# Loading the FFN's first weights ahead of the query weights in a one-core decode kernel

## The chip, the cores and the metric

The kernel runs on one core of a Trainium2 chip. The core has five engines, each with its own stream of instructions: TensorE (PE), which multiplies matrices and writes its results to PSUM; VectorE (DVE); ScalarE (ACT); GpSimd (POOL); and SyncE (SP), which here does nothing but issue DMA transfers. The engines wait for each other, and for transfers, through semaphores. Sixteen DMA engines carry data from HBM to the on-chip memory (SBUF). Transfers issued by one engine go through one queue.

The metric is device time in microseconds (us) of one execution; lower is better. The median of 3 runs of the kernel before is 675.64 us (675.47 to 675.78).

## The reference

One decoding step for two sequences: attention over a long cache, beside a small FFN, mixed by a gate. The cut version:

```python
B, D = 2, 448;  H, Sk, Dh = 16, 4096, 256;  F = 1792      # all float32

g = sigmoid((x * gate_w).sum(-1))                          # x: [B, 1, D]
q = (x @ wq) as [B, H, 1, Dh]                              # wq: [D, H*Dh]
p = softmax(q . k_cache * Dh**-0.5)                        # k_cache, v_cache: [B, H, Sk, Dh]
a = (p . v_cache) as [B, 1, H*Dh] @ wo                     # wo: [H*Dh, D]
h = relu(x @ w1 + b1) ** 2                                 # w1: [D, F]
b = h @ w2 + b2                                            # w2: [F, D]
out = g * a + (1 - g) * b                                  # [B, 1, D]
```

The caches are 134 MB each, and every byte of them is used once. wq is 7.3 MB, w1 and w2 3.2 MB each, wo 7.3 MB.

## The kernel before

**Rounds.** The cache is worked through in 16 rounds. A round is one sequence and two heads (`rounds`, `of_round`): its keys are a tile of 128 partitions by 64 KB, its values likewise. Keys go in turn to two buffers, `kp[0]` and `kp[1]`; values go to one buffer, `vp` (the last rounds use `kp` as well).

**One round's work.** The vector engine multiplies the keys with the round's query, which lies copied to all partitions (`times_q`, L439), and sums each row (`row_sums`, L444). Each is done in two halves of 128x8192 elements, so a round has four long vector instructions (`rest`). `maximum` takes the largest score: a vector reduction, two PE matmuls that carry it to all partitions of a head, and a second reduction in `softmax`, after which ACT takes the exponentials into `pw`. `values` (64 matmul instructions) multiplies `pw` with the values. The query tile of a round is made by `make_q`: two PE matmuls pick a row of `qs` and spread it, and ACT copies it out of PSUM to one of three tiles.

**Queue of loads.** All large loads are issued by SP through `load` (L271), in the order in which the program writes them. SP waits before an issue until the place that the transfer overwrites has been read for the last time, and whatever is written behind waits as well. So the keys of round i + 2 wait until the vector engine has ended round i, because they share a buffer, and the values of round i + 1 until PE has ended `values` of round i.

**The start.** wq, w1 and the first values all use `vp`, one after the other. SP's order is: wq (L300), the keys of round 0 (`load_k(0)`, L399), w1 (L424), the keys of round 1 (L433), and then, in the loop of L638, values of round 0, keys of round 2, values of round 1, keys of round 3. Meanwhile ACT issues small loads of x, gate_w, b2 and b1 (L309 to L321) in its own queue, into a corner of `kp[1]`. From x a small PE matmul and four vector instructions make `xT` (L367 to L373), the operand by which `times_x` (L375) multiplies wq or w1. Then PE has three more small matmuls in its order: the gate's (L390), b2's (L392) and b1's (L394); b1's writes the PSUM bank `ph`, which the vector engine reads at L395. After these, PE multiplies with wq (L421, into the bank `po1`), ACT copies the result to `qs` (L422), the first two queries are made (L425, L426), and PE multiplies with w1 (L429, into the bank `ph`); ACT copies that to `shared` (L431). `ffn_turn` (L634) transposes it on PE after the first softmax, and `ffn_square` (L648) adds b1, squares and gates it in the first pass of the loop.

**The order of work on an engine** is the order in which the program writes its operations (`op`). Waits are worked out from the places that each operation reads and writes. PE runs rounds 0 to 11 in hardware loops of four passes (`flow.loop`); the vector engine, ACT and SP have them written out.

**The end.** The last rounds, the projection by wo and the FFN's second layer follow, with w2 loaded last of all.

Of the kernel before, what the change touches and what calls it, by code (L numbers as in the profile page):

```python
# [6 lines left out]
AF = mybir.ActivationFunctionType  # L7
# [3 lines left out]
PE, ACT, DVE, POOL, SP = "PE", "ACT", "DVE", "POOL", "SP"  # L11
# [12 lines left out]
class Flow:  # L24
# [22 lines left out]
    def op(self, eng, fn, r=(), w=(), give=None, take=(), dma=None):  # L47
        proc = dma or eng
        looped = eng == PE and self.body is not None
        o = Op(proc, eng, fn, give, looped)  # L50
        mine = self.ops.setdefault(proc, [])
        mine.append(o)
        o.n = len(mine)
        know = self.know[eng]
        for t in take:
            p = self.tokens[t].pop(0)
            o.takes.append((t, 16 if p.proc not in self.eng else 1))
            self.learn(know, p)
        need = {}
        for writes, regions in ((False, r), (True, w)):  # L60
            for name, lo, hi in map(self.span, regions):
                for p, a, b, wrote in self.seen.setdefault(name, []):
                    if a >= hi or b <= lo or not (wrote or writes):
                        continue
                    if p.proc == proc == PE:
                        continue
                    if know.get(p.proc, 0) < p.n and need.get(p.proc, p).n <= p.n:
                        need[p.proc] = p
        for p in sorted(need.values(), key=lambda p: -p.n):
            if know.get(p.proc, 0) >= p.n:  # L70
                continue
            assert not looped, (eng, p.proc, p.n, r, w)
            while p.give and p.proc in self.eng:
                later = [q for q in self.ops[p.proc][p.n:] if not q.give and q is not o]
                assert later, (eng, p.proc, p.n, r, w)
                p = later[0]
            p.inc = True
            o.waits.append(p)
            self.learn(know, p)
        for writes, regions in ((False, r), (True, w)):  # L80
            for name, lo, hi in map(self.span, regions):
                at = self.seen.setdefault(name, [])
                if writes:
                    at[:] = [x for x in at if not (lo <= x[1] and x[2] <= hi)]
                at.append((o, lo, hi, writes))
        o.know = dict(know)
        if give:
            self.tokens.setdefault(give, []).append(o)
        if looped:
            if self.passes == 1:  # L90
                self.body.append(o)
            else:
                first = self.body[self.at]
                assert first.takes == o.takes and not o.waits, (first.takes, o.takes)
                self.at += 1
        else:
            self.order[eng].append(o)
        return o
# [84 lines left out]
def gated_mix_kernel(nc, x, k_cache, v_cache, wq, wo, w1, b1, w2, b2, gate_w, out):  # L183
    P = 128
    B, H, S, DH = k_cache.shape
    D = x.shape[-1]
    F = w1.shape[1]
    N = H * DH
    XR = 7
# [10 lines left out]
    QB = 512  # L200
    NQ = N // QB
# [11 lines left out]
    scale = DH ** -0.5  # L213

    flow = Flow(nc)
    op = flow.op

    def sb(name, *shape):
        return nc.alloc_sbuf_tensor(name, shape, F32).ap()

    def bank(name):
        return nc.alloc_psum_tensor(name, (P, 512), F32).ap()
# [3 lines left out]
    vp = sb("vp", P, NK * DH)  # L226
# [10 lines left out]
    xT = sb("xT", P, 2, XC, 2, B)  # L237
# [5 lines left out]
    qs = sb("qs", P, QB)  # L243
# [14 lines left out]
    po_t = [bank(f"po{n}") for n in range(2)]  # L258
# [7 lines left out]
    def rows(t):  # L266
        return t.rearrange("p (j d) -> p j d", d=DH)

    def load(eng, sem, dst, src, w, r=(), give=None):
        e = flow.eng[eng]  # L270
        op(eng, lambda: e.dma_start(dst, src), r=r, w=w, dma=sem, give=give)  # L271

    def place(t, lo=0, hi=NK * DH):
        return ("vp" if t is vp else "kp1" if t is kp[1] else "kp0", lo, hi)
# [7 lines left out]
    def of_round(src, i):  # L282
        b, n = rounds[i]
        return src[b, 2 * n:2 * n + 2].rearrange("h (p j) d -> (h p) j d", p=PH)

    def load_k(i, lo=0, hi=NK):
        t = kp[i % 2]
        load(SP, f"k{i % 2}_{lo}", rows(t)[:, lo:hi, :], of_round(k_cache, i)[:, lo:hi, :], [place(t, lo * DH, hi * DH)])
# [7 lines left out]
        return t  # L296

    by7 = "(r k) (s n) -> (r k s) n"
    wq_t = vp[:, :D * N // P]
    load(SP, "wq", wq_t, wq.rearrange(by7, k=XR, s=2).rearrange("(p k) n -> p (k n)", k=XR), [place(vp, 0, D * N // P)])  # L300

    start_at = kp[1][:B, :4 * D + XC * P]

# [19 lines left out]
    v_, s_, t_, g_ = nc.vector, nc.scalar, nc.tensor, nc.gpsimd  # L323
# [36 lines left out]
    def mms(calls):  # L360
        def run():
            for out_, lhsT, rhs, start, stop in calls:
                i = t_.matmul(out_, lhsT, rhs, start=start, stop=stop, skip_group_check=True)  # L363
            return i
        return run

    op(PE, mms([(pxv[:, c, :], xr[:, c].rearrange("b r s -> b (r s)"), ident[:B, :B], True, True) for c in range(XC)]),  # L367
       r=[xr_r, "ident"], w=["sm"])
# [6 lines left out]
    def times_x(out_, t, width, n):  # L375
        calls = []
        for a in range(XR):
            c, half = divmod(a, 2)
            for k in range(n):
                calls.append((out_[32 * k:32 * k + 2 * B, :width], xT[:, half, c].rearrange("p s b -> p (s b)"),  # L380
                              t[:, (a * n + k) * width:(a * n + k + 1) * width], a == 0, a == XR - 1))
        return mms(calls)
# [20 lines left out]
    def col(i):  # L403
        b, n = rounds[i]
        a, k = divmod(n, NQ // 2)
        r = 32 * k + B * a + b
        return ident[:, r:r + 1]

    def make_q(i, token=False):
        c = sel if token else col(i)  # L410
        op(PE, mms([(pq[k * PH:(k + 1) * PH, :DH], c.to_broadcast([P, PH]), qs[:, k * DH:(k + 1) * DH], True, True)
                    for k in range(2)]), r=["qs", "sel" if token else "ident"], w=["pq"], take=["q"] if token else ())
        t = q_t[i % 3]
        q_of[i] = t
        op(ACT, lambda: s_.activation(t, pq[:, :DH], AF.Copy), r=["pq"], w=[f"q{i % 3}"])  # L415
# [2 lines left out]
        c = col(i)  # L418
        op(ACT, lambda: s_.activation(sel, c, AF.Copy), r=["ident"], w=["sel"], give="q")

    op(PE, times_x(po_t[1], wq_t, QB, NQ // 2), r=["xT", place(vp, 0, D * N // P)], w=["po1"])  # L421
    op(ACT, lambda: s_.activation(qs, po_t[1], AF.Copy, scale=scale), r=["po1"], w=["qs"])  # L422
    w1_t = vp[:, :D * F // P]
    load(SP, "w1", w1_t, w1.rearrange(by7, k=XR, s=2).rearrange("(p k) n -> p (k n)", k=XR), [place(vp, 0, D * F // P)])  # L424
    make_q(0)  # L425
    make_q(1)  # L426

    h_sb = shared[:2 * B, :F // 2]
    op(PE, times_x(ph, w1_t, D, FB // 2), r=["xT", place(vp, 0, D * F // P)], w=["ph"])  # L429
    for k in range(FB // 2):  # L430
        op(ACT, lambda k=k: s_.activation(h_sb[:, k * D:(k + 1) * D], ph[32 * k:32 * k + 2 * B, :D], AF.Copy),  # L431
           r=["ph"], w=[("shared", k * D, (k + 1) * D)])
    load_k(1)  # L433

    def times_q(i, half, lo, hi):
# [320 lines left out]
```

## Time and profile before

| what | value |
|---|---|
| median of 3 runs | 675.64 us (675.47 to 675.78) |
| the profiled execution | 675.83 us, of which the span from its first to its last instruction is 674.4 us |
| DMA, share of 16 engines, large loads | 99.3% |
| moved | 289.73 MB, mean 430 GB/s |
| vector engine busy | 571.1 us (85%) |
| PE busy | 254.9 us (38%) |
| ACT busy | 43.5 us (6%) |
| mean granted clock of TensorE | 0.656 |

The profile is one execution. All its times count from the first instruction. A line of its timeline has the start in us, the duration in us, the engine, the line of the kernel, the operation, the tile written and the tiles read, and the number of instructions that were merged; in square brackets stands the engine's idle time just before and what ended it. "SPq" or "ACTq" marks the issue of a transfer; its duration is that of the issuing instruction, not of the transfer. Most PE instructions have the line L363, which is that of a helper: they are told apart by their tiles. w1 and w2 both show as `in_B_w_dram`, b1 and b2 as `in_B_b_dram`. "PEld" is the loading of a matmul's stationary operand. A line of the view by stretches has the stretch, its length, each engine's busy time and number of instructions, then the granted TensorE clock, the mean busy share of the 16 DMA engines, and GB/s.

### The profile page before, as it was taken

What the parts mean: (1) busy time and instruction counts of PE and PEld (TensorE: products, weight loads), DVE (VectorE), ACT (ScalarE), POOL (GpSimd) and SP (SyncE); (2) the same over time, 40 slices, a digit from 0 to 9 for tenths busy, and PEclk for the clock granted to TensorE, in tenths of its full rate; (3) what the DMA queues carried; (4) which work ended last, traced back from release to release, by engine and by line L of the source; (5) the groups of instructions that cost most, each with busy time, mean ns of one, the idle gap of its engine ahead of it and who ended that gap; (6) DMA issues with size and microseconds to landing.
All of it is one profiled execution on the core that took longest, in us unless ns stands there. A gap on an engine that the chain in (4) does not pass through costs nothing.

```text
span 674.4 us, 3918 instructions
## 1 busy us (share of the span) xinstructions
PE 254.9 (38%) x1716; PEld 87.4 (13%) x1716; DVE 571.1 (85%) x147; ACT 43.5 (6%) x145; POOL 0.7 (0%) x6
## 2 busy tenths in 40 slices
PE   2612350512305761140505455050321580421598
PEld 1100210100001510010101311010000140000223
DVE  3069999999999895989979896897979899999930
ACT  0001000010100201010000201000010110000000
POOL 0000000000000000000000000000000000000000
PEclk9957585655758577585856578565575856565789
DMA  9999999999999999999999999999999999999997
GB/s 382 428 439 436 436 435 435 435 435 436 435 435 431 424 436 435 435 435 435 435 435 431 424 436 435 435 431 435 435 435 435 415 445 435 435 436 435 410 438 325
DMA packets 6679, 289.73 MB, mean 430 GB/s; under 512 B 766, under 2 KB 908, under 8 KB 1548
## 3 DMA queue, kind: packets, MB, share of 16 engines
q1 hardware_dynamic: 6616, 289.54, 99.3%
q8 instruction: 9, 0.15, 0.1%
q10 hardware_dynamic: 52, 0.02, 0.0%
q14 instruction: 2, 0.02, 0.0%
HBM read 289.56 MB, written 0.01 MB: 429 GB/s over the span
## 4 chain that ended last, share of the span: by engine, by line
DMA 43%; DVE 26%; PE 3%; SPq 0%; issue 0%; DVEq 0%
DMA kp<-in_A_k_cache_dram 26%; DVE s L444 13%; DVE kp L439 13%; DMA vp<-in_A_v_cache_dram 11%; DMA kp<-in_B_w_dram 6%; PE po L363 3%; SPq L271 0%; PE fin L363 0%; PE mt L363 0%; DVE shared L682 0%; DVEq L155 0%; DVE nb L466 0%
## 5 line engine op out<-in xcount | busy, mean ns | idle before, releaser
L439 DVE TENSOR_TENSOR kp<-kp,q 128x8192 f32<-128x8192 f32 (+2 forms) x34 | 278.2, 8183 | 48.8 <-DMA kp<-in_A_k_cache_dram 48.8
L444 DVE TENSOR_REDUCE s<-kp 128x32 f32<-128x8192 f32 x32 | 277.9, 8686 | 1.1
L363 PE MATMUL po<-vp,pw 128*16 128x512 f32 (+1 forms) x960 | 135.3, 726 | 225.5 <-PEq L153 205.3
L363 PEld LDWEIGHTS po<-vp,pw 128*16 128x16 f32 (+1 forms) x960 | 31.0, 110 | 326.5 <-issue 303.4
L363 PE MATMUL mt<-ident,m 128*64 128x64 f32 x64 | 7.2, 318 | 142.0 <-PEq L153 89.2
L363 PE MATMUL sm<-rl,shared 128*128 128x8 f32 (+1 forms) x120 | 25.3, 347 | 9.4 <-ACT shared L524 8.1
L363 PE MATMUL acc<-wo,oTw 128*2 128x448 f32 x48 | 26.1, 714 | 2.5 <-ACT oTw L533 2.5
L363 PEld LDWEIGHTS sm<-rl,shared 128*128 128x128 f32 x120 | 24.7, 313 | 11.6 <-DVE rl L497 4.6
L363 PEld LDWEIGHTS mt<-ident,m 128*64 128x64 f32 x64 | 4.8, 191 | 155.9 <-issue 101.1
L485 ACT ACTIVATE pw<-zero 128x128 f32<-128x128 f32 x12 | 3.7, 311 | 322.6 <-PE po L363 322.6
L473 ACT ACTIVATE pw<-s,nb 64x64 f32<-64x64 f32 x32 | 11.1, 348 | 168.6 <-DVE nb L466 168.4
L682 DVE COPY shared<-fin 64x112 f32<-64x112 f32 x1 | 0.3, 268 | 19.7 <-PE fin L363 19.7
L363 PE MATMUL ph<-vp,xT 128*4 128x448 f32 x28 | 8.2, 756 | 15.6 <-DMA vp<-in_B_w_dram 15.6
L363 PE MATMUL po<-kp,pw 128*8 128x512 f32 x64 | 10.1, 787 | 5.9 <-DMA kp<-in_A_v_cache_dram 5.9
L466 DVE TENSOR_REDUCE nb<-mt 128x1 f32<-128x64 f32 x16 | 3.6, 224 | 10.2 <-PE mt L363 10.2
L363 PE MATMUL pq<-qs,sel 128*64 128x256 f32 x48 | 12.2, 594 | 0.0
L363 PE MATMUL po<-vp,xT 128*4 128x512 f32 x56 | 8.7, 786 | 1.5 <-DMA vp<-in_A_wq_dram 1.5
L415 ACT ACTIVATE q<-pq 128x256 f32<-128x256 f32 x16 | 6.1, 384 | 21.5 <-PE pq L363 21.3
L495 DVE RECIPROCAL rc<-sm 128x8 f32<-128x8 f32 (+1 forms) x5 | 1.0, 196 | 7.7 <-PE sm L363 7.7
L363 PEld LDWEIGHTS acc<-wo,oTw 128*2 128x2 f32 x48 | 4.7, 102 | 21.7 <-issue 18.9
L524 ACT ACTIVATE shared<-po 128x512 f32<-128x512 f32 x12 | 6.5, 592 | 11.4 <-PE sm L363 11.4
L363 PE MATMUL ph<-kp,ones_pp 128*16 128x512 f32 x48 | 6.7, 593 | 0.0
(79 smaller groups left out, 77.8 us busy)
## 6 DMA issues: line engine op xcount, KB each, us to landing
vp<-in_A_wq_dram SPq DMA_DIRECT2D x1, 7168.0 KB, 19.7
wo<-in_A_wo_dram SPq DMA_DIRECT2D x3, 1792.0 KB, 46.2
vp<-in_A_v_cache_dram SPq DMA_DIRECT2D x1, 4096.0 KB, 23.9
vp<-in_B_w_dram SPq DMA_DIRECT2D x1, 3136.0 KB, 18.0
vp<-in_A_v_cache_dram SPq DMA_DIRECT2D x1, 3072.0 KB, 30.8
wo<-in_A_wo_dram SPq DMA_DIRECT2D x2, 896.0 KB, 33.6
kp<-in_B_w_dram SPq DMA_DIRECT2D x1, 1792.0 KB, 36.6
vp<-in_A_v_cache_dram SPq DMA_DIRECT2D x1, 1024.0 KB, 32.8
```

Source lines behind the costliest of these rows:

```text
L363: i = t_.matmul(out_, lhsT, rhs, start=start, stop=stop, skip_group_check=True)
L415: op(ACT, lambda: s_.activation(t, pq[:, :DH], AF.Copy), r=["pq"], w=[f"q{i % 3}"])
L439: vec(lambda: v_.tensor_tensor(kt, kt, q.unsqueeze(1).to_broadcast([P, hi - lo, DH]), op=ALU.mult), at + [f"q{i % 3}"], at)
L444: vec(lambda: v_.tensor_reduce(s[:, at], rows(t)[:, at, :], axis=AX.X, op=ALU.add), [place(t, half * HALF, (half + 1) * HALF)], [(f"s{i % ...
L466: vec(lambda: v_.tensor_reduce(nb, mt[:, :PH], axis=AX.X, op=ALU.max, negate=True), ["mt"], [f"nb{i % 2}"])
L473: op(ACT, lambda: s_.activation(pw[at, :, 2 * c:2 * c + 2], s[at].rearrange("p (m s) -> p m s", s=2), AF.Exp, bias=nb[at], accum_out=rs[at ...
L485: op(ACT, lambda: s_.activation(at, zero.unsqueeze(2).unsqueeze(3).to_broadcast([P, NK // 2, 2, 2]), AF.Copy), r=["zero"], w=[("pw0", 2 * ...
L495: vec(lambda: v_.reciprocal(c, sm[:, :B * n].rearrange("p (k b) -> p k b", b=B)), ["sm"], ["rc"])
L524: op(ACT, lambda s=s, lo=lo: s_.activation(o_w[:, s], pv[:, s, lo:lo + HJ // 2].unsqueeze(2).to_broadcast([P, HJ // 2, HG, HP]), AF.Copy), ...
L682: vec(lambda: v_.tensor_copy(t[:PH, :DQ], fin[:PH, :DQ]), ["fin"], [at[0]])
```

## The change

w1 and wq change places. w1 is loaded first, at the start of the program, and wq in its place later, when PE has read w1. On PE and on ACT, the FFN's first layer now stands in front of q, and the first two queries stand behind both. The keys of round 0 still come second and those of round 1 fourth. Sizes, buffers and the operations themselves are the same.

```diff
@@ -296,8 +296,8 @@
     by7 = "(r k) (s n) -> (r k s) n"
-    wq_t = vp[:, :D * N // P]
-    load(SP, "wq", wq_t, wq.rearrange(by7, k=XR, s=2).rearrange("(p k) n -> p (k n)", k=XR), [place(vp, 0, D * N // P)])
+    w1_t = vp[:, :D * F // P]
+    load(SP, "w1", w1_t, w1.rearrange(by7, k=XR, s=2).rearrange("(p k) n -> p (k n)", k=XR), [place(vp, 0, D * F // P)])
...
@@ -418,18 +418,18 @@
-    op(PE, times_x(po_t[1], wq_t, QB, NQ // 2), r=["xT", place(vp, 0, D * N // P)], w=["po1"])
-    op(ACT, lambda: s_.activation(qs, po_t[1], AF.Copy, scale=scale), r=["po1"], w=["qs"])
-    w1_t = vp[:, :D * F // P]
-    load(SP, "w1", w1_t, w1.rearrange(by7, k=XR, s=2).rearrange("(p k) n -> p (k n)", k=XR), [place(vp, 0, D * F // P)])
-    make_q(0)
-    make_q(1)
-
     h_sb = shared[:2 * B, :F // 2]
     op(PE, times_x(ph, w1_t, D, FB // 2), r=["xT", place(vp, 0, D * F // P)], w=["ph"])
     for k in range(FB // 2):
         op(ACT, lambda k=k: s_.activation(h_sb[:, k * D:(k + 1) * D], ph[32 * k:32 * k + 2 * B, :D], AF.Copy),
            r=["ph"], w=[("shared", k * D, (k + 1) * D)])
+    wq_t = vp[:, :D * N // P]
+    load(SP, "wq", wq_t, wq.rearrange(by7, k=XR, s=2).rearrange("(p k) n -> p (k n)", k=XR), [place(vp, 0, D * N // P)])
+    op(PE, times_x(po_t[1], wq_t, QB, NQ // 2), r=["xT", place(vp, 0, D * N // P)], w=["po1"])
+    op(ACT, lambda: s_.activation(qs, po_t[1], AF.Copy, scale=scale), r=["po1"], w=["qs"])
+    make_q(0)
+    make_q(1)
+
     load_k(1)
```

## The prediction

> **What bounds the kernel now.** I read the page from the top: busy shares, the forty slices, the chain that ended last.
>
> ```profile
> span 674.4 us, 3918 instructions
> ...
> DMA  9999999999999999999999999999999999999997
> GB/s 382 428 439 436 436 435 435 435 435 436 435 435 431 424 436 435 435 435 435 435 435 431 424 436 435 435 431 435 435 435 435 415 445 435 435 436 435 410 438 325
> ...
> DMA 43%; DVE 26%; PE 3%; SPq 0%; issue 0%; DVEq 0%
> ```
>
> The DMA engines are busy in every slice but the last, at a flat 435 GB/s, and the chain is made of transfers and of the vector work that lets the next one be issued. In the view by stretches the long middle is full (share 1.00):
>
> ```profile
> 2.00:87.00 85.00, 28.14 (x174) 10.54 (x178) 51.58 (x33) 6.66 (x14) 0.00 (x0) 0.72 0.98 425
> 110.00:670.00 560.00, 215.39 (x1404) 73.04 (x1408) 495.25 (x110) 36.23 (x129) 0.00 (x0) 0.64 1.00 433
> ```
>
> So the time is the bytes at 435 GB/s, plus a start and a tail. The change moves no byte in or out. It can cost only where it lets the DMA queue run empty, and a hole of that kind is paid in full, since no idle DMA time behind it could take it up. The question is thus which issue comes too late. The timeline of the first 130 us gives the loads in SP's order (SPq rows are issues) and the work they wait for:
>
> ```profile
> 0.74 0.40 SPq L271 DMA_DIRECT2D vp<-in_A_wq_dram  x1
> ...
> 1.20 0.42 SPq L271 DMA_DIRECT2D kp<-in_A_k_cache_dram  x1
> ...
> 29.26 0.33 SPq L271 DMA_DIRECT2D vp<-in_B_w_dram  x1
> ...
> 29.63 0.44 SPq L271 DMA_DIRECT2D kp<-in_A_k_cache_dram  x1
> ...
> 39.89 8.69 DVE L439 TENSOR_TENSOR kp<-kp,q 128x8192 f32<-128x8192 f32 x1 [20.27 <-DMA kp<-in_A_k_cache_dram]
> ...
> 47.35 8.16 PE L363 MATMUL ph<-vp,xT 128*4 128x448 f32 x28 [15.65 <-DMA vp<-in_B_w_dram]
> ...
> 55.55 0.33 SPq L271 DMA_DIRECT2D vp<-in_A_v_cache_dram  x1
> ...
> 65.94 8.69 DVE L444 TENSOR_REDUCE s<-kp 128x32 f32<-128x8192 f32 x1
> ...
> 74.65 0.33 SPq L271 DMA_DIRECT2D kp<-in_A_k_cache_dram  x1
> ...
> 86.95 8.76 PE L363 MATMUL po<-vp,pw 128*16 128x512 f32 x64 [6.94 <-PEq L153]
> ...
> 95.77 0.33 SPq L271 DMA_DIRECT2D vp<-in_A_v_cache_dram  x1
> ...
> 125.55 5.32 PE L363 MATMUL po<-vp,pw 128*16 128x512 f32 x24 [12.68 <-PEq L153]
> ```
>
> The order is wq, k0, w1, k1, v0, k2, v1, k3. A key or value load is 128 partitions of 64 KB, 8.39 MB, so 19.3 us at 435 GB/s; between v0 and v1 (the starts of their matmuls, 86.95 and 125.55) lie 38.60 us, two such loads. They land in the order of issue: w1, issued at 29.26, is used at 47.35, after k0 (39.89). **The issue to watch is k2's**, at 74.65: it waits until the last reduction over k0 has ended (65.94 + 8.69 = 74.63), because it goes into the same buffer. v0 lands at 86.95, so k2 stands in the queue 12.3 us before its turn. That is all the cover there is.
>
> **The change, part by part.** *First: w1's matmuls and wq's issue.* With w1 first, 7168 - 3136 KB = 4.13 MB less lie ahead of k0, 9.5 us: w1 lands at about 20.49 - 9.5 = 11.0 (20.49 is where wq is used, quoted below), k0 at 39.89 - 9.5 = 30.4. wq is now issued when w1's matmuls end, and they stand behind small matmuls that need ACT's loads (gate_w, b2, b1):
>
> ```profile
> 7.37 0.22 DVE L373 TENSOR_SCALAR xT<-sm,eo 128x6 f32<-128x6 f32 x1
> ...
> 9.61 0.61 DVE L384 SCALAR_TENSOR_TENSOR kp<-kp 2x448 f32<-2x448 f32 x1 [2.02 <-DMA kp<-in_gate_w_dram]
> ...
> 10.96 0.59 PE L363 MATMUL sm<-gd,ones_pp 2*128 2x4 f32 x2 [4.12 <-DVE gd L389]
> ...
> 13.99 1.65 PE L363 MATMUL acc<-kp,gd 2*2 2x448 f32 x2 [2.44 <-DMA kp<-in_B_b_dram]
> ...
> 18.24 0.77 PE L363 MATMUL ph<-kp 16*128 16x112 f32 x2 [2.61 <-DMA kp<-in_B_b_dram]
> ...
> 19.04 0.27 DVE L395 TENSOR_TENSOR kp<-ph,m_i 128x112 f32<-128x112 f32 x1 [7.30 <-PE ph L363]
> ```
>
> The three land 4.3 us apart. The DMA view of the first 18.5 us tells why:
>
> ```profile
> q1 hardware_dynamic: 128, 7.34, 94.9%
> ```
>
> wq is 128 packets, 8 for each of 16 engines, of 56 KB, so about 16.9 / 8 = 2.1 us each; 4.3 us is two. Each small load thus seems to take two turns, one of SP's packets going between. w1 too should be 8 packets per engine, but of 24.5 KB, 0.93 us: a load every 1.9 us; gate_w's 9.61 - 0.74 = 8.9 us after the first issue shrink in the same ratio to 3.9, so gate_w by about 5, b1 by about 9. Then the vector engine goes on at 7.6, and PE as before: 1.35 us to the gd matmul (10.96 - 9.61), 0.6, 1.65, 0.77, then 0.3 for L395, which must read ph before w1's matmuls overwrite it: they start near 12.4 and end at 20.6. wq is issued then, 9.8 us before k0 lands. **Cost nothing, hidden by k0's transfer.** Without that cover wq's delay would come on top. Should b1's and b2's turns fall among k0's 64 KB packets (4.8 us per load), b1 comes at about 14 and wq's issue at 24, still in time.
>
> *Second: q.* Ahead of wq's landing now lie w1 and k0, ahead of w1's lay wq and k0: the same three loads, so wq lands where w1 did, at 47.35 instead of 20.49. From there to the first q:
>
> ```profile
> 20.49 8.69 PE L363 MATMUL po<-vp,xT 128*4 128x512 f32 x56 [1.49 <-DMA vp<-in_A_wq_dram]
> 21.30 0.15 PEld L363 LDWEIGHTS po<-vp,xT 128*4 128x4 f32 x4 [0.70 <-issue]
> ...
> 25.57 0.11 PEld L363 LDWEIGHTS po<-vp,xT 128*4 128x4 f32 x4 [0.70 <-issue]
> 26.01 0.10 PEld L363 LDWEIGHTS po<-vp,xT 128*4 128x4 f32 x4 [0.33 <-issue]
> ...
> 29.26 0.60 ACT L422 ACTIVATE qs<-po 128x512 f32<-128x512 f32 x1 [18.80 <-PE po L363]
> ...
> 30.61 0.38 ACT L415 ACTIVATE q<-pq 128x256 f32<-128x256 f32 x1 [0.75 <-PE pq L363]
> ```
>
> From 20.49 to 30.99 are 10.50 us, so q0 is ready at 57.85, and the vector engine, which had started k0 at 39.89, starts it there: **18.0 us late**. The 14 groups of 4 matmuls run at 0.85 us each up to 25.57 and at 0.44 after; all of them slow would take 12.0 us, all quick 6.0, so this term has bounds of +3.3 and -2.7 (the granted clock over 2 to 87 us, quoted above, is 0.72: some of each). I take 8.69, because PE is idle ahead of wq in both.
>
> The Trainium skill (TensorE: Matmul & The Clock Gate, Part 1: The HAM clock gate) says that an idle PE runs at half clock and is released after about 3.4 us of activity. By that, four slow groups and ten quick ones would make 7.8 us and the time about 0.9 us less; here the slow stretch is 5.1 us, and I go by the row.
>
> *Third: k2's issue.* The vector work on k0 takes 74.65 - 39.89 = 34.76 us (two products, two reductions), none of it changed. It ends at 57.85 + 34.76 = 92.6, and k2 is issued there. v0 is issued when q's matmuls end, 47.35 + 8.69 = 56.0, with k1 in the queue till about 66.6, so it lands at 86.95 as before. **The queue is then empty**: k2's 18.0 us of delay less 12.3 of cover leave 5.7, and a transfer that meets an empty queue also pays its start. The row that shows one is the first load's, on the page:
>
> ```profile
> vp<-in_A_wq_dram SPq DMA_DIRECT2D x1, 7168.0 KB, 19.7
> ```
>
> 7.34 MB at 435 GB/s are 16.9 us, so 2.8 of the 19.7 are start and completion. The lower bound is the 0.33 us of the issuing instruction (row at 74.65). I take 2.8, as the only load that found an empty queue; some of it may belong to the program's start. k2 then lands at 92.6 + 2.8 + 19.3 = 114.7; before, at 125.55 - 19.3 = 106.25. **The stream is 8.5 us late from there on.**
>
> *Fourth: what is late next.* Behind k2 stand v1 (waits for the values matmuls of round 0) and k3 (for the vector work of round 1):
>
> ```profile
> 75.34 3.62 PE L363 MATMUL sm<-ident,shared 4*64 4x4 f32 x56
> ...
> 78.89 1.12 PE L363 MATMUL pq<-qs,ident 128*64 128x256 f32 x4
> ...
> 110.35 0.33 SPq L271 DMA_DIRECT2D kp<-in_A_k_cache_dram  x1
> ```
>
> PE is through with the maxima, the FFN's transposes and the third q 5.4 us after the vector engine (80.01 - 74.63), so at 98.0; values take 8.8 more, v1 is issued at 106.8, 7.9 us before k2 lands. What entering the loop costs PE is hidden now in its 6.94 us of idleness; it may be 0 to 6.94, and only its upper end would open a second hole. k3 is issued 35.7 us after k2 (110.35 - 74.65), at 128.3; v1 lands at 134.0. The cover is 5.7 us and grows by 38.6 - 35.7 = 2.9 each round. One hole, then. Nothing earns it back: FFN's first layer done earlier frees nothing that is waited for.
>
> **Sum**: 0 (wq's issue) + 8.5 (k2) + 0 (the rest). The profiled execution took 675.83 (span 674.4 and 1.4 around it), 0.2 above the median of 675.64; 8.5 on the median is **684.1**.
>
> **The rivals.** *wq too late.* If ACT's small loads got no turn until k0 is through, b1 would come at 30.4, w1's matmuls would start near 31.5 and end at 39.7, wq would land at 39.7 + 2.8 + 16.9 = 59.4, 12 us late, with k2's hole behind it: 684.1 + 12.0 = 696.1. It decides if w1's matmuls start after about 20.8. Against it stand the 4.3 us steps above. The Trainium skill (DMA: Bandwidth & Descriptors, Queues, rings and completion order) says that an engine drains a whole packet of some 9 to 17 descriptors from one queue before it turns to another. If each of the profile's packets were one descriptor, w1's 8 and some of k0's would pass in one turn, and this rival would come true; the 4.3 us steps speak for turns of a single one.
>
> *A second hole at v1*, if the loop's entry costs PE nearly 7 us: v1's issue at 113.8 is some 0.5 us too late for an unbroken queue, and part of a start comes on top: up to 2 us, 686.1.
>
> *Not slower: wq passes the first keys.* If the queue served wq, issued at 20.6, ahead of what is left of k0, it would land at 20.6 + 19.7 = 40.3, q0 would be ready at 50.8 and k0 there by 47.4. The vector work would end at 85.6, and k2 would just follow v0 without a hole: 675.7. It decides at a vector start of 50.8: k2's issue must come about 1.4 us before 86.95. Against it: before, w1 waited out k0 in the same queue.
>
> **How the numbers follow.** Forecast with its spread in q's matmuls and the start: 0.84. Second hole: 0.05. wq late: 0.06. Not slower: 0.03. Something that I don't see and that makes it faster: 0.02. The range goes from the quickest q (684.1 - 2.7 = 681.4; the cheapest start gives 684.1 - 2.5 = 681.6) to the slowest q (684.1 + 3.3 = 687.4), which takes in the second hole and leaves out 696 and 675.7. 0.2% is 1.35 us, about what a measurement of this kernel can tell from no change: slower 0.95, same 0.03, faster 0.02.
>
> **What would show it.** In the changed kernel's timeline: w1's matmuls from about 12 to 21, wq's issue behind them and well before 29, q's matmuls from about 47.4, the first vector product over keys near 58, k2's issue near 92.6 with k1's and v0's loads through at 87, and a slice of lower GB/s there alone. The vector engine should wait less for later keys than it does now. It is wrong if the DMA share has no dent at 86 to 95, if there is one near 30, or if a second one follows.

## The result, and the profile after

The changed kernel takes 684.35 us (684.22 to 685.06, 4 runs) against 675.65 (675.47 to 675.78, 4 runs): a ratio of 1.0129, 95% interval 1.0117 to 1.0141. It is 8.7 us slower. The profiled execution is the longest of the four, 685.06 us with a span of 683.6, so the rows below are up to 0.7 us later than those of a median run.

The page of the changed kernel, with the vector product over the keys (busy time, mean duration in ns, then its engine's idle time before it and what ended it):

```profile
span 683.6 us, 3918 instructions
...
DMA  9999869999999999999999999999999999999997
...
q1 hardware_dynamic: 6616, 289.54, 98.2%
...
DMA 40%; DVE 25%; PE 4%; issue 0%; SPq 0%; DVEq 0%
...
L439 DVE TENSOR_TENSOR kp<-kp,q 128x8192 f32<-128x8192 f32 (+2 forms) x34 | 278.2, 8182 | 65.2 <-ACT q L415 45.1
```

Bytes and instructions are the same. What is new is a dent in the fifth and sixth slice. The same row of the kernel before:

```profile
L439 DVE TENSOR_TENSOR kp<-kp,q 128x8192 f32<-128x8192 f32 (+2 forms) x34 | 278.2, 8183 | 48.8 <-DMA kp<-in_A_k_cache_dram 48.8
```

The vector engine now waits 45.1 us for the first query, and not for keys. The remaining 65.2 - 45.1 = 20.1 us are to be set against 48.8 - 20.3 = 28.5 us of the kernel before (its first wait, for k0, was 20.3).

The timeline of the changed kernel, start to second values:

```profile
10.93 0.76 PE L363 MATMUL ph<-kp 16*128 16x112 f32 x2
...
12.06 8.15 PE L363 MATMUL ph<-vp,xT 128*4 128x448 f32 x28 [0.37 <-DVE kp L395]
...
20.26 0.33 SPq L271 DMA_DIRECT2D vp<-in_A_wq_dram  x1
...
47.04 8.48 PE L363 MATMUL po<-vp,xT 128*4 128x512 f32 x56 [26.83 <-DMA vp<-in_A_wq_dram]
...
57.37 8.69 DVE L439 TENSOR_TENSOR kp<-kp,q 128x8192 f32<-128x8192 f32 x1 [45.06 <-ACT q L415]
...
83.42 8.69 DVE L444 TENSOR_REDUCE s<-kp 128x32 f32<-128x8192 f32 x1
92.13 0.33 SPq L271 DMA_DIRECT2D kp<-in_A_k_cache_dram  x1
...
97.42 8.06 PE L363 MATMUL po<-vp,pw 128*16 128x512 f32 x64
...
105.56 0.33 SPq L271 DMA_DIRECT2D vp<-in_A_v_cache_dram  x1
...
127.83 0.33 SPq L271 DMA_DIRECT2D kp<-in_A_k_cache_dram  x1
...
134.66 9.91 PE L363 MATMUL po<-vp,pw 128*16 128x512 f32 x64 [4.30 <-PEq L153]
```

And the view by stretches of the same kernel (last two columns: DMA share and GB/s; a packet counts where it starts):

```profile
2.00:84.50 82.50, 22.65 (x106) 6.30 (x106) 32.15 (x29) 5.20 (x8) 0.00 (x0) 0.68 1.00 430
84.50:93.00 8.50, 0.59 (x8) 0.47 (x8) 7.88 (x3) 0.00 (x0) 0.00 (x0) 0.50 0.00 0
93.00:97.00 4.00, 4.00 (x60) 3.65 (x60) 4.00 (x2) 0.88 (x4) 0.00 (x0) 0.50 1.37 524
97.00:680.00 583.00, 220.59 (x1500) 74.92 (x1497) 525.56 (x113) 37.12 (x132) 0.00 (x0) 0.64 1.00 432
```

Read together: from 84.5 to 93 us no packet of any transfer starts. SP issues k2 at 92.13, just behind the last reduction over k0 (83.42 + 8.69 = 92.11), and the stream goes on at 93 and is never interrupted again. The values of round 1, which land behind k2, are used at 134.66 instead of 125.55, 9.1 us later; the span has grown by 9.2. All of the loss is there. The vector engine, 17.5 us late at its start (57.37 - 39.89), ends its last reduction over keys 9.2 us late (646.13 + 8.69 instead of 636.89 + 8.69), because it waits 28.5 - 20.1 = 8.4 us less afterwards.

### The profile page after: what moved, and what is told of

It is laid out like the page before. It is cut to its first block, busy times and chain, and to the rows that moved or that the text cites. A ratio compares the mean times of both kernels' runs of the same rounds, so it can differ in the third digit from the quotient of the medians.

```text
span 683.6 us, 3918 instructions
## 1 busy us (share of the span) xinstructions
PE 249.7 (37%) x1716; PEld 86.4 (13%) x1716; DVE 570.9 (84%) x147; ACT 43.4 (6%) x145; POOL 0.7 (0%) x6
## 4 chain that ended last, share of the span: by engine, by line
DMA 40%; DVE 25%; PE 4%; issue 0%; SPq 0%; DVEq 0%
DMA kp<-in_A_k_cache_dram 25%; DMA vp<-in_A_v_cache_dram 16%; DVE s L444 13%; DVE kp L439 13%; PE po L363 3%; PE fin L363 1%; PE ph L363 0%; PE sm L363 0%; SPq L271 0%; PE mt L363 0%; DVE shared L682 0%; DVEq L155 0%; DVE nb L466 0%
## 5 line engine op out<-in xcount | busy, mean ns | idle before, releaser
L439 DVE TENSOR_TENSOR kp<-kp,q 128x8192 f32<-128x8192 f32 (+2 forms) x34 | 278.2, 8182 | 65.2 <-ACT q L415 45.1
L363 PE MATMUL po<-vp,pw 128*16 128x512 f32 (+1 forms) x960 | 133.2, 713 | 180.0 <-PEq L153 159.6
```

The source lines that it names most:

```text
L439: vec(lambda: v_.tensor_tensor(kt, kt, q.unsqueeze(1).to_broadcast([P, hi - lo, DH]), op=ALU.mult), at + [f"q{i % 3}"], at)
```

## The experiments

**Theory A**: the time is lost because k2's issue waits for the vector work on k0, which waits for q. **Theory B**: the changed order of loads and of PE work costs the time by itself, and the vector engine's delay is harmless. Each run was timed against the kernel before on the same chip (675.6 to 675.73 us); times are medians. The lead of an issue is the time by which it comes ahead of the landing of the load in front of it. For k2 it is counted here up to 86.95, where the values of v0 are used in the kernel before; the expectations of runs 5, 6 and 8 count up to 84.7, when the first DMA engine is through with v0, so their leads are 2.2 us shorter.

**1 to 3. The old order with a late vector engine.** The kernel before gets extra reductions ahead of the work on k0, with results that the real ones overwrite. One, one and a half, and two:

```diff
+    for _ in range(2):          # the run with two
+        row_sums(0, 0)
     rest(0, 0, 0)
```

> The kernel before with one more reduction over the first half of the first keys, ahead of the work on them: 8.7 us more on the vector engine, nothing else moved. Theory A (the time is lost in a hole of the DMA stream, because k2's issue waits for the vector work on k0): k2 is issued at 83.3 instead of 74.65, still ahead of v0's end at about 86.4, so no hole and 675.6 us. Theory B (the vector engine's delay is harmless as such; the changed order of loads and PE work costs the time): 675.6 too. A third view, that any vector delay at the start lengthens the chain one for one: 684.3.

> The kernel before with one and a half such reductions more, 13.0 us on the vector engine. A: k2 is issued at 87.7, about 1.3 us after v0's last packets; with the start of a transfer into an empty queue as in the changed kernel (8.7 us lost at an issue of 92.13), 4.3 us lost, 679.9 us; if a start costs nothing beyond the delay, some 2 us, 677.6. B: 675.6.

> The kernel before with two such reductions more, 17.4 us: k2's issue comes at 92.05, as late as in the changed kernel (92.13), with the old order of loads and of PE work. A: 684.3 us, the changed kernel's own time. B: 675.6.

Measured: **677.85, 680.08 and 684.60 us** (ratios 1.003, interval 1.0017 to 1.0042; 1.0065, 1.0049 to 1.0082; 1.0134, 1.0117 to 1.0151). With two reductions k2's issue and the values of round 1 stand in the timeline at

```profile
91.63 0.33 SPq L271 DMA_DIRECT2D kp<-in_A_k_cache_dram  x1
...
134.06 9.91 PE L363 MATMUL po<-vp,pw 128*16 128x512 f32 x64 [4.19 <-PEq L153]
```

and its view by stretches has the changed kernel's hole, with wq loaded first as of old:

```profile
84.50:92.50 8.00, 0.59 (x8) 0.48 (x8) 7.38 (x3) 0.00 (x0) 0.00 (x0) 0.50 0.00 0
```

With one and a half the two rows are

```profile
87.50 0.33 SPq L271 DMA_DIRECT2D kp<-in_A_k_cache_dram  x1
...
129.92 9.99 PE L363 MATMUL po<-vp,pw 128*16 128x512 f32 x64 [4.19 <-PEq L153]
```

So a late vector engine alone gives the changed kernel's time, and B falls. But one reduction, for which A too expected nothing, cost 2.2 us. Its rows:

```profile
83.19 0.33 SPq L271 DMA_DIRECT2D kp<-in_A_k_cache_dram  x1
...
128.09 8.95 PE L363 MATMUL po<-vp,pw 128*16 128x512 f32 x64 [6.68 <-PEq L153]
```

k2 was issued 3.8 us before v0's landing (86.95 in the kernel before), and yet v1 came 2.5 us late. Here are 85 to 90 us, where k2's first packets run, in the kernel before and with one reduction:

```profile
85.00:90.00 5.00, 3.05 (x16) 0.75 (x20) 5.00 (x1) 0.00 (x0) 0.00 (x0) 0.50 1.03 446
```

```profile
85.00:90.00 5.00, 5.00 (x54) 3.02 (x56) 5.00 (x1) 0.73 (x4) 0.00 (x0) 0.50 0.93 367
```

Share times 16 engines times 64 KB, divided by the rate, gives 2.42 us per packet before and 2.66 with one reduction; the DMA engines were idle for only 0.3 us on average. The trace records 16 completions for a load. For v1 the median one came 0.9 us later than in the kernel before (124.82 instead of 123.97), the last one, for which PE waits, 2.5 us later (127.96 instead of 125.42).

**4. Three reductions.**

> The kernel before with three more reductions over the first half of the first keys, 26.1 us: k2's issue at 100.7. A: the hole grows one for one, 684.35 + 8.6 = 693.0 us, and no second one opens. B: 675.6. If the vector engine's spare time (15% of the span) took up part of it later: well under 693.

Measured: **693.25 us** (1.026, 1.0243 to 1.0277). k2's issue and the values of round 1:

```profile
100.67 0.33 SPq L271 DMA_DIRECT2D kp<-in_A_k_cache_dram  x1
...
143.27 9.01 PE L363 MATMUL po<-vp,pw 128*16 128x512 f32 x64 [4.37 <-PEq L153]
```

From an issue at 87.50 (one and a half) to one at 100.67 the issue moves by 13.17 us and the time by 693.25 - 680.08 = 13.17. Past v0's landing, each microsecond of delay is paid in full.

**5 and 6. Where the loss begins.** Either the lead of an issue must be longer than thought (L), or every vector delay costs a part of itself (V). Half and three quarters of a reduction:

```diff
+    vec(lambda: v_.tensor_reduce(s_t[0][:, :16], rows(kp[0])[:, :16, :], axis=AX.X, op=ALU.add),
+        [place(kp[0], 0, 16 * DH)], [("s0", 0, 1)])          # 24 in place of 16 for three quarters
     rest(0, 0, 0)
```

> The kernel before with half a reduction more (4.35 us on the vector engine), so k2's issue at 79.0, 5.7 us before the first engine ends v0 (84.7). With a whole one (issue 83.2, 1.5 us before) 2.2 us were lost. Theory L (the loss there is a short lead: a transfer issued so late finds some DMA engines waiting for it): 675.6 us. Theory V (any vector delay costs a share of itself, here a quarter): 676.7.

> The kernel before with three quarters of a reduction more (6.5 us), k2's issue at 81.2, a lead of 3.5 us. L: at the edge, 675.6 to 676.6 us. V: 677.2.

Measured: **675.79 and 675.75 us** (1.0002, 0.9992 to 1.0011; 0.9999, 0.9990 to 1.0009). With three quarters, k2 is issued here and v1 is in time:

```profile
81.23 0.33 SPq L271 DMA_DIRECT2D kp<-in_A_k_cache_dram  x1
...
125.64 8.44 PE L363 MATMUL po<-vp,pw 128*16 128x512 f32 x64 [6.18 <-PEq L153]
```

5.7 us ahead of v0's landing is enough, 3.8 us is not. V falls, and L holds as to where the loss begins. As to how, DMA engines that wait are the smaller part in run 1: its packets were slow, and the last engine fell behind the others.

**7 and 8. w1 first, without wq's wait.** w1 goes to the second key buffer, so that wq can be issued at once, and the loads are w1, wq, k0, k1, v0:

```diff
-    w1_t = vp[:, :D * F // P]
+    w1_t = kp[1][:, 4096:4096 + D * F // P]
...
+    wq_t = vp[:, :D * N // P]
+    load(SP, "wq", wq_t, ..., [place(vp, 0, D * N // P)])
...
-    wq_t = vp[:, :D * N // P]
-    load(SP, "wq", wq_t, ..., [place(vp, 0, D * N // P)])
     op(PE, times_x(po_t[1], wq_t, QB, NQ // 2), ...)
```

> The changed kernel with w1 put into the second key buffer, so that wq needs not wait for w1's matmuls: the loads are w1, wq, k0, k1, v0. FFN's first layer stays in front of q. A: wq lands near 28, k0 near 47.3, and the vector engine starts there, below the 50.8 from which a hole opens; k2 is issued near 82.1, no hole: 675.6 us. B (w1 first, with the FFN in front of q, costs by itself): 684.4.

The second of the two also loads k2 in halves, as in run 9:

> w1 in the second key buffer, loads w1, wq, k0, k1, v0 as in the run before that lost 2.1 us, and k2 loaded in two halves, the first issued near 65.4. L: the lead is 19 us, 675.6 us. V, or a cost of the order w1, wq, k0 by itself: 677.8 as without the halves.

Measured: **677.79 us** (1.003, 1.0018 to 1.0043), then **675.73 us** (1.0000, 0.9991 to 1.0010). In the first, k2 is issued with 4.1 us to go before 86.95:

```profile
82.83 0.33 SPq L271 DMA_DIRECT2D kp<-in_A_k_cache_dram  x1
...
128.37 9.02 PE L365 MATMUL po<-vp,pw 128*16 128x512 f32 x64 [7.30 <-PEq L153]
```

In the second, the two issues of k2 start at 65.64 (merged into one row), with the vector work at the same times, and nothing is lost:

```profile
65.64 17.65 SPq L271 DMA_DIRECT2D kp<-in_A_k_cache_dram  x2
...
125.60 9.39 PE L365 MATMUL po<-vp,pw 128*16 128x512 f32 x64 [4.41 <-PEq L153]
```

So w1 first and FFN's layer in front of q cost nothing in themselves, in this order of loads (w1, wq, k0), and the 2.1 us of the first were the short lead again.

**9 to 11. The changed kernel with keys in halves.** The first half can be issued when the vector engine is through with the first half of the old keys:

```diff
         vt = load_v(i, vp)
-        load_k(i + 2)
+        if i == 0:                 # i < 2 and i < 6 in the other two runs
+            load_k(i + 2, 0, J)
+            load_k(i + 2, J, NK)
+        else:
+            load_k(i + 2)
         values(i, vt)
```

> The changed kernel with k2 loaded in two halves, the first issued when the vector engine has done the first half of k0. Order of loads, buffers and PE work are the changed kernel's. A: the first half is issued at about 74.8, well ahead of 86.4, and its 9.6 us cover the wait for the second (issued at 92.2, needed at 96), so no hole: 675.6 us. B: 684.4, since the order is unchanged.

> The changed kernel with k2 and k3 loaded in two halves each; with k2 alone in halves it took 681.9 us, with two smaller holes, near 105 (v1 issued at 105.7, when k2 had run out) and near 126 (k3 issued at 126.8, when v1 had). If those two are what is left: the hole near 126 goes, k3's first half being issued near 109, and some 2 to 3.5 us remain for v1's: 677.6 to 679.1. If the order costs by itself: 681.9.

> The changed kernel with k2 to k7 loaded in two halves each. With k2 and k3 alone in halves it took 680.4 us, and its trace has two places where the DMA engines ran short: 104 to 107 (v1 issued at 105.7) and 164 to 167 (k4 issued at 164.5, with v2 just through). If those two make up the whole loss, the second goes and v1's remains: v1 lands some 2 us late, 677.6 to 678.2 us. If the changed order costs anything else: above 679.

Measured: **681.93, 680.43 and 680.09 us** (1.0096, 1.0079 to 1.0113; 1.0066, 1.0049 to 1.0083; 1.0064, 1.0047 to 1.0081). All three expectations were too low. In the first, k2's hole is gone, and two others stand in its place: v1's issue, behind the values of round 0, and k3's, behind the vector work of round 1, come when the queue has run out:

```profile
105.73 0.33 SPq L271 DMA_DIRECT2D vp<-in_A_v_cache_dram  x1
126.82 0.33 SPq L271 DMA_DIRECT2D kp<-in_A_k_cache_dram  x1
```

The changed kernel issues them at nearly the same times (105.56, 127.83), but there the hole ahead had moved the stream back by 9 us and covered them. With k2 to k7 in halves v1's hole remains; the stretch in its view where almost no packet starts is

```profile
104.00:106.50 2.50, 1.68 (x16) 0.22 (x8) 2.50 (x1) 0.31 (x1) 0.00 (x0) 1.00 0.06 26
```

and the values of rounds 3 and 5 start in it, and in the kernel before, at

```profile
205.75 8.64 PE L363 MATMUL po<-vp,pw 128*16 128x512 f32 x64 [3.69 <-PEq L153]
...
288.56 9.89 PE L363 MATMUL po<-vp,pw 128*16 128x512 f32 x64 [13.16 <-PEq L153]
```

```profile
202.75 8.89 PE L363 MATMUL po<-vp,pw 128*16 128x512 f32 x64 [18.31 <-PEq L153]
...
284.53 8.96 PE L363 MATMUL po<-vp,pw 128*16 128x512 f32 x64 [26.65 <-PEq L153]
```

3.0 us late, then 4.0. v1 itself lands 2.2 us late, as expected (the last of its 16 completions is at 127.64, in the kernel before at 125.42), but the median completion is 3.2 us late (127.2 instead of 124.0): right behind the hole the last engine lags little, and by round 3 it lags more again. The hole thus costs about 3, not the 2 that was expected. A fourth microsecond comes between the two rounds, and the median time is 4.4 us above the kernel before; what makes up these last 1.4 us stays open. That the order by itself takes them is not excluded, though run 8, with w1 first and no loss, speaks against it.

**12. wq's wait made long.** In the changed kernel, b1 goes through SP's queue behind the first keys, so that w1's matmuls, and wq's issue behind them, come late:

```diff
-    load(ACT, "b1", b1r, b1.rearrange("(r n) -> r n", r=BR), [b1r_at])
...
+    load_k(0)
+    load(SP, "b1", b1r, b1.rearrange("(r n) -> r n", r=BR), [b1r_at])
     op(PE, mms([(ph[:, :BI * FC], e16, b1r, True, True)]), r=[e16_at, b1r_at], w=["ph"])
```

> The changed kernel with b1 loaded through SP's queue behind the first keys, so that it lands near 30.5 and w1's matmuls, which stand behind b1's on PE, start near 31.5 and end near 39.7. A: wq is issued into an empty queue at 39.8 and lands near 59.5, 12 us later than in the changed kernel, and k2's hole comes on top: 684.4 + 12 = 696.4 us, two holes in the DMA share. If holes at the start were covered by one another (the later one takes up the first), 688 or less.

Measured: **696.31 us** (1.03, 1.0283 to 1.0317). Two holes, in its view by stretches:

```profile
29.00:40.00 11.00, 8.72 (x30) 1.96 (x30) 0.55 (x2) 0.54 (x2) 0.00 (x0) 1.00 0.00 1
...
96.00:104.50 8.50, 0.12 (x2) 0.12 (x4) 8.29 (x2) 0.00 (x0) 0.00 (x0) 0.50 0.00 0
```

and in its timeline k2's issue and the values of round 1:

```profile
104.10 0.33 SPq L271 DMA_DIRECT2D kp<-in_A_k_cache_dram  x1
...
146.76 9.95 PE L363 MATMUL po<-vp,pw 128*16 128x512 f32 x64 [4.43 <-PEq L153]
```

The holes add up, because the late q moves with the stream and keeps k2 just as late behind v0. This is the price of the cover that hides wq's wait in the changed kernel.

## Why the prediction was right, point by point

**wq's wait costs nothing: right.** w1's matmuls began at 12.06 (12.4 forecast) and wq's issue came at 20.26 (20.6), 9.8 us ahead of k0's last completion (30.10). b1's small matmul began at 10.93, so b1 was there by then. The Trainium skill's rule of 9 to 17 descriptors per turn (DMA: Bandwidth & Descriptors, Queues, rings and completion order) would have made b1 wait for part of k0, if each packet of the profile were one descriptor. The trace shows no such wait. Run 12 showed that this rival, had it come true, would have cost what was worked out for it: 12.0 us, 696.31 measured against 696.1.

**q is 18 us late: right.** q's matmuls began at 47.04 (47.35), took 8.48 (8.69), and the vector engine began at 57.37 (57.85), so 17.5 us late. The granted clock was 0.50 from their start until 51.7, for 4.7 us, and 1.00 after that. The 7.8 us that the Trainium skill's clock rule (TensorE: Matmul & The Clock Gate, Part 1: The HAM clock gate) would give did not come.

**k2's hole: right in its place and in its sum, off in two terms that partly cancel.** k2's issue came at 92.13 instead of 92.6. The start of a transfer into an empty queue was put at 2.8 us, from the first load of the program; v1's use at 134.66, less two loads of 19.3 and the issue at 92.13, makes it 3.9, and the same sum gives 3.8 for one and a half reductions (k2 at 87.50, v1 at 129.92) and for two, and 4.0 for three. -0.5 and +1.1 on 8.5 give 9.1, which is what the profiled execution shows; the median run lost 8.7. That the sum comes so near is partly luck: its two errors have opposite signs. The missing 1.1 us is no slower start. It is mostly the lag of the last DMA engine, 0.6 us at wq's landing in the kernel before and 1.7 at v1's here, as the last section shows.

**One hole only: right.** values began at 97.42, at once behind the third q, so that entering the loop cost PE nothing that is seen here, and v1 and k3 were issued before the stream needed them. Runs 9 to 11 showed why: the hole itself bought them that time.

**The point from which a hole opens: wrong.** The rival "not slower" put it at a vector start of 50.8, with k2's issue 1.4 us ahead of v0's landing. The vector engine started at 48.08 in run 7 and 2.1 us were lost. The lead that an issue needs lies between 4.1 and 5.7 us. The same 1.4 us is in the 20.8 us that "wq too late" allows for w1's matmuls (30.4 - 1.4 - 8.2) and in the second hole at v1, so both limits lie too late. It did not matter for the forecast, as the changed kernel is far past the point at k2 and well ahead of it at wq (9.8 us) and at v1 (issued at 105.56, k2's last completion at 115.22).

## What to carry to other kernels

In a kernel whose DMA queue never runs empty, the order of the loads is free only as long as every issue keeps its lead. To price a reordering, find for each issue the instruction that it waits for, work out how late that one becomes, and set it against the landing of the load in front. Here a lead of 5.7 us cost nothing and one of about 4 us cost 2; an issue past the landing cost its lateness and some 4 us on top. A delay that eats one lead eats the next ones too: when the first hole is closed, look at the next two issues before you count the gain. Keep what leads to the vector engine's first work (here q) at the front.

## What the runs showed of the hardware

A transfer issued by SP while its predecessor was still running lost time unless it was issued well ahead: none with 5.7 us to the predecessor's landing, 2.1 and 2.2 us with 4.1 and 3.8.

Keys that found the queue empty cost 3.8 to 4.1 us beyond bytes at 435 GB/s, from k2's issue to the use of v1 behind it, in each of five kernels (the changed one, runs 2, 3 and 4, and the second hole of run 12). wq cost less: 2.8 us as the first load of the kernel before, and 2.5 in the first hole of run 12, where 16.9 of the 19.36 us from its issue to its use are bytes:

```profile
39.45 0.33 SPq L271 DMA_DIRECT2D vp<-in_A_wq_dram  x1
...
58.81 8.69 PE L363 MATMUL po<-vp,xT 128*4 128x512 f32 x56 [19.41 <-DMA vp<-in_A_wq_dram]
```

Finer stretches of the changed kernel show the end of v0 and the start of k2, issued at 92.13:

```profile
82.30:82.90 0.60, 0.00 (x0) 0.00 (x0) 0.60 (x1) 0.00 (x0) 0.00 (x0) 0.50 3.78 1638
82.90:83.80 0.90, 0.00 (x0) 0.00 (x0) 0.86 (x2) 0.00 (x0) 0.00 (x0) 0.50 0.00 0
83.80:84.00 0.20, 0.00 (x0) 0.00 (x0) 0.20 (x1) 0.00 (x0) 0.00 (x0) 0.50 0.78 328
...
92.10:93.00 0.90, 0.59 (x8) 0.47 (x8) 0.28 (x3) 0.00 (x0) 0.00 (x0) 0.50 0.00 0
93.00:93.60 0.60, 0.60 (x14) 0.60 (x14) 0.60 (x2) 0.40 (x2) 0.00 (x0) 0.50 5.09 1748
93.60:95.90 2.30, 2.30 (x41) 2.30 (x42) 2.30 (x1) 0.48 (x3) 0.00 (x0) 0.50 0.00 0
95.90:96.90 1.00, 1.00 (x14) 0.75 (x12) 1.00 (x1) 0.00 (x0) 0.00 (x0) 0.50 2.42 1049
```

Of the 16 last packets of v0, 15 start before 82.90 (0.60 us at 1638 GB/s are 15 packets of 64 KB) and end by 85.3; the last one starts near 83.9 and ends at 86.4. All 16 first packets of k2 start within the stretch from 93.00 (0.60 us at 1748 GB/s are 1.05 MB), 0.9 to 1.5 us after the issue, and they take 0.60 x 5.09 = 3.05 us each against 2.42 for the next ones, in the last stretch. The Trainium skill (DMA: Bandwidth & Descriptors, Specifications) gives some 0.6 us to the first byte for this path. The trace's 0.9 to 1.5 us to the first packets are longer than that.

So about 1.1 us of the 3.9 pass before the first packets, and 0.6 go to their slowness. Most of the rest is at the end of the sum: of v1's 16 completions in the trace the median one comes at 132.86 and the last at 134.52, 1.7 us later, and PE begins at 134.66. Such a lag is there in an unbroken stream too (v0 in the kernel before: 85.30 and 86.82), so it is no cost of the start. It means that 15 of the 16 DMA engines ran out of work more than a microsecond before the point that is called v0's landing here. At wq it is smaller (19.81 and 20.45 in the kernel before, 58.42 and 58.77 in run 12's first hole). Some 0.5 us is not separated, and why one engine lags was not tested.
